# Two MLP layers on one Trainium2 core: seven block products for eight over batch pairs, with a fixed order of engines

## The chip, the cores and the metric

The kernel runs on one core of a Trainium2 chip. The time is the device time of one execution in microseconds. A core has a matrix engine (TensorE, PE in the rows; its weight loads are PEld), VectorE (DVE), ScalarE (ACT), GpSimd (POOL), and a sync engine (SP) that here only issues transfers.

## What is computed

Attention over 4 batches and 12 heads feeds two layers of the same width; all arithmetic is judged at float32.

```python
# q, k, v: (4, 12, 448, 64)
q_n, k_n = rmsnorm(q, g_q), rmsnorm(k, g_k)
attn = softmax(q_n @ k_n.T / 8) ; x = attn @ v          # -> (4, 448, 768)
xn = (x - mean) / sqrt(var + 1e-6) * g_ln               # layer 0
x  = x + relu(xn @ w_ch1) @ w_ch2                       # 768 -> 3072 -> 768
u  = x + (x.T @ U @ V).T                                # layer 1: mixing over tokens, rank 32
out = u + relu(u @ w_ch1') @ w_ch2'
```

The weights arrive as 64-bit floats and are narrowed on the core by integer operations on their two halves.

## The kernel before

Attention goes head by head with a software pipeline (`attention`, lines 229 to 499); beside it run, as generators that are advanced one step per stage, the scaling of finished batches (`scale`), the layer norm (`ln_stats`, `ln_apply`) and the first weights (`early`). The result of batch b lies transposed in `x[b]`, six blocks of 128 features by 448 tokens.

Each operand of the layers' matmuls is kept as a high and a low part, and every product is three matmuls: high by high, low by high, high by low. A layer is 12 steps of two hidden blocks (`G = 2`). In each step all four batches go by in turn. For a batch, `h_unit` makes one hidden block of 128 by 448 (6 blocks of inputs x 3 = 18 matmuls, L591), ACT writes its high part (L595) and VectorE its low part (L596). `o_unit` makes one of the six output blocks from the two hidden blocks of the batch before (2 x 3 = 6 matmuls, L605), and VectorE adds it to `x` (L607). That is 36 + 36 matmuls for a batch in a step, each 128x128 weights by 448 columns.

The weights of a step are used by all four batches: `w_load` fetches a tile of 128x768 in two halves from SP's queue (L517), `w_narrow` makes float32 of it (`narrow`, L80 to L87: one ACT operation for each half, two VectorE operations on the whole, two for each half), and `w_split` makes high and low parts on ACT (L531) and POOL (L532).

All tiles in PSUM come from one pool of eight banks. The scheduler of the framework orders each engine's instructions, within what the program pins (`keep_in_program_order`). In `mlps` each unit is followed by one to four steps of a side generator: the rest of batch 3's scaling and layer norm during the first step, and `mix` (the token mixing of layer 1) as soon as a batch has left layer 0. `mix` transposes `x` in groups of three blocks (L557), multiplies by U and by V (L566, L575), adds into `x` (L576) and splits the sum for layer 1 (L577, L578).

Of the kernel before, what the change touches and what calls it, by code (L numbers as in the profile page):

```python
# [11 lines left out]
U32 = mybir.dt.uint32  # L12
AF = mybir.ActivationFunctionType
# [13 lines left out]
NCH = NF // G  # L27
EPS = 1e-6
NX = 4
SN = 2  # L30
OS = "smpabn"
NB = 2
DL = 3
# [6 lines left out]

CLAMP = struct.unpack("<f", struct.pack("<I", 0x30100000))[0]

# [5 lines left out]
def build(tc, qkv, gg, g_ln, w1a, w2a, w1b, w2b, u_in, v_in, out):  # L48
    nc = tc.nc
    V, A, PL, PE = nc.vector, nc.scalar, nc.gpsimd, nc.tensor  # L50
    with ExitStack() as es:
        cpool = es.enter_context(tc.tile_pool(name="const", bufs=1))
        xpool = es.enter_context(tc.tile_pool(name="x", bufs=1))
        psum = es.enter_context(tc.tile_pool(name="ps", bufs=5, space=bass.MemoryType.PSUM))
        lpool = es.enter_context(tc.tile_pool(name="lt", bufs=4))
        rpool = es.enter_context(tc.tile_pool(name="raw", bufs=4))
        fpool = es.enter_context(tc.tile_pool(name="wf", bufs=2))
# [3 lines left out]
        cnt = [0]  # L61

        def bank(name, tag="ps"):
            cnt[0] += 1
            return psum.tile([P, 512], F32, tag=tag, name=f"{name}{cnt[0]}", bufs=8)
# [5 lines left out]
        def narrow(raws, f, hold=False):  # L71

            fu = f.bitcast(U32)
            parts, at = [], 0
            for r in raws:
                n = r.shape[1]
                parts.append((r[:, :, 1], r[:, :, 0], slice(at, at + n)))
                at += n
            for hi, lo, n in parts:
                A.activation(f[:, n], hi.bitcast(F32), AF.Abs, scale=2.0 ** -16)  # L80
            ins = V.tensor_scalar(f, f, CLAMP, None, ALU.max)  # L81
            if hold:
                tc.keep_in_program_order(ins)
            V.tensor_scalar(fu, fu, 4, 1, ALU.logical_shift_left, ALU.logical_shift_right)
            for hi, lo, n in parts:
                V.scalar_tensor_tensor(fu[:, n], lo, 29, fu[:, n], ALU.logical_shift_right, ALU.bitwise_or)  # L86
                V.scalar_tensor_tensor(fu[:, n], hi, 0x80000000, fu[:, n], ALU.bitwise_and, ALU.bitwise_or)  # L87
# [46 lines left out]
        xh, xl = {}, {}  # L134

        def norm_tiles(b, pool, again=True):
            if b in xh and not again:
                return xh[b], xl[b]
            xh[b] = pool.tile([P, KD, S], F32R, tag=f"xh{b}", name=f"xh{b}_{cnt[0]}")
            xl[b] = pool.tile([P, KD, S], F32R, tag=f"xl{b}", name=f"xl{b}_{cnt[0]}")  # L140
            return xh[b], xl[b]

        pin = tc.keep_in_program_order
# [9 lines left out]
        def ln_stats(b, pool=None):  # L153
# [6 lines left out]
            if b < B - 1:  # L160
                xs = lt("xs")
                for c in range(NC):
                    cs = slice(c * CP, (c + 1) * CP)
                    V.tensor_reduce(xs[:, cs], x[b][:, :, cs].rearrange("p k n -> p n k"), AX.X, ALU.add)
                    yield
                yield
                parts = [xs]
            else:
                for _ in range(3):
                    yield  # L170
                parts = [x[b][:, k, :] for k in range(KD)]
# [9 lines left out]
            for n in range(KD + 1 + lag):  # L181
# [3 lines left out]
                if n < KD:  # L185
                    odd = b == B - 1 and n % 2
                    sqs[n] = acc if n == 0 else bank("sq")[:, :S] if odd else lt(f"sq{n}", pool)
                    (V if b == B - 1 and n % 2 else PL).tensor_tensor(sqs[n], x[b][:, n, :], mu, ALU.subtract)
# [346 lines left out]
        def early():  # L535
            for u in range(2):
                w_load(u)
# [186 lines left out]
```

## Time and profile before

| | |
|---|---|
| three runs | 1827.44, 1832.0, 1840.74 us (median 1832.0) |
| profiled execution, span of its instructions | 1826.3 us; the page gives no time of its own beside it |
| busy: PE, DVE, ACT, POOL | 97%, 61%, 31%, 24% |
| chain that ended last | 79% PE, of it the two layers' matmuls (L605 and L591) 38% each |
| DMA | 116.52 MB, mean 64 GB/s |

Busy is the share of the span in which an engine executed. A matmul's own duration overlaps the next one's, so what a matmul costs in a row of them is read from the chain of waits, where each step is followed back to what released it. The granted clock is given as a share of full speed.

### The profile page before, as it was taken

What the parts mean: (1) busy time and instruction counts of PE and PEld (TensorE: products, weight loads), DVE (VectorE), ACT (ScalarE), POOL (GpSimd) and SP (SyncE); (2) the same over time, 40 slices, a digit from 0 to 9 for tenths busy, and PEclk for the clock granted to TensorE, in tenths of its full rate; (3) what the DMA queues carried; (4) which work ended last, traced back from release to release, by engine and by line L of the source; (5) the groups of instructions that cost most, each with busy time, mean ns of one, the idle gap of its engine ahead of it and who ended that gap; (6) DMA issues with size and microseconds to landing.
All of it is one profiled execution on the core that took longest, in us unless ns stands there. A gap on an engine that the chain in (4) does not pass through costs nothing.

```text
span 1826.3 us, 22748 instructions
## 1 busy us (share of the span) xinstructions
PE 1776.4 (97%) x8690; PEld 1556.3 (85%) x8690; DVE 1108.7 (61%) x1942; ACT 565.8 (31%) x1147; POOL 430.1 (24%) x307
## 2 busy tenths in 40 slices
PE   5999998899999999999999999999999999999999
PEld 4666665588999999999999988999999999999998
DVE  6768787869655646465555676555555466454633
ACT  6786776633121221122121244121221112111210
POOL 5445667433110110111010133210110101110100
PEclk9999999999999999999999999999999999999999
DMA  4453433412212211121112201111212122111103
GB/s 107 107 121 72 107 84 96 126 37 90 84 36 70 70 35 54 50 70 51 54 37 68 69 27 44 35 47 58 70 35 70 36 69 70 35 52 52 35 1 121
DMA packets 72990, 116.52 MB, mean 64 GB/s; under 512 B 30065, under 2 KB 42929, under 8 KB 72881
## 3 DMA queue, kind: packets, MB, share of 16 engines
q1 hardware_dynamic: 45232, 99.92, 19.0%
q10 hardware_dynamic: 27648, 15.14, 3.3%
q8 instruction: 68, 1.11, 0.3%
q14 instruction: 42, 0.34, 0.1%
HBM read 98.35 MB, written 5.68 MB: 57 GB/s over the span
## 4 chain that ended last, share of the span: by engine, by line
PE 79%; POOL 2%; DVE 2%; issue 2%; DMA 0%; ACT 0%; SPq 0%; POOLq 0%; DVEq 0%; ACTq 0%
PE o L605 38%; PE h L591 38%; PE po L399 1%; PE t L566 1%; PE xt L557 0%; POOL w L532 0%; DVE m L349 0%; POOL ln_d L222 0%; POOL xl L217 0%; DVE ln_acc L184 0%; POOL raw L287 0%; SPq L456 0%; DVE wf L86 0%; POOL xl L578 0%; PE mu L174 0%
## 5 line engine op out<-in xcount | busy, mean ns | idle before, releaser
L591 PE MATMUL h<-xh,w 128*128 128x448 f32 x2304 | 656.7, 366 | 2.6 <-ACT xh L216 2.6
L605 PE MATMUL o<-hh,w 128*128 128x448 f32 x2304 | 657.0, 366 | 0.0
L591 PEld LDWEIGHTS h<-xh,w 128*128 128x128 f32 x2304 | 433.7, 188 | 37.5 <-ACT xh L216 3.0
L605 PEld LDWEIGHTS o<-hh,w 128*128 128x128 f32 x2304 | 432.8, 188 | 35.0 <-issue 1.1
L607 DVE TENSOR_TENSOR x<-x,o 128x448 f32<-128x448 f32 x576 | 349.9, 617 | 158.8 <-PE o L605 155.6
L532 POOL TENSOR_TENSOR w<-wf,w 128x768 fp32r<-128x768 f32 x96 | 183.1, 1917 | 1056.8 <-ACT w L531 1056.8
L591 PE MATMUL h<-xl,w 128*128 128x448 f32 x1152 | 422.0, 366 | 0.6 <-POOL xl L217 0.5
L605 PE MATMUL o<-hl,w 128*128 128x448 f32 x1152 | 421.1, 366 | 0.0
L595 ACT ACTIVATE hh<-h 128x448 fp32r<-128x448 f32 x192 | 103.7, 540 | 794.3 <-PE h L591 794.3
L596 DVE SCALAR_TENSOR_TENSOR hl<-h,hh 128x448 fp32r<-128x448 f32 x192 | 119.3, 622 | 322.6 <-ACT hh L595 322.5
L591 PEld LDWEIGHTS h<-xl,w 128*128 128x128 f32 x1152 | 216.9, 188 | 19.3 <-POOL xl L217 2.2
L605 PEld LDWEIGHTS o<-hl,w 128*128 128x128 f32 x1152 | 216.7, 188 | 17.2
L399 PE MATMUL po<-p,vf 112*128 112x448 f32 x384 | 178.2, 547 | 2.1 <-DVE m L349 2.1
L349 DVE TENSOR_REDUCE m<-pm 112x1 f32<-112x448 f32 x192 | 118.0, 618 | 48.7 <-PE pm L348 48.0
L81 DVE TENSOR_SCALAR wf<-wf 128x768 f32<-128x768 f32 x96 | 67.9, 707 | 128.0 <-ACT wf L80 121.7
L80 ACT ACTIVATE wf<-wr 128x384 f32<-128x384 f32 x192 | 96.8, 549 | 148.0 <-POOL w L532 147.4
L86 DVE SCALAR_TENSOR_TENSOR wf<-wr,wf 128x384 uint32<-128x384 uint32 x192 | 122.9, 661 | 1.7
L531 ACT CAST w<-wf 128x768 fp32r<-128x768 f32 x96 | 77.8, 831 | 130.4 <-PE o L605 116.9
L87 DVE SCALAR_TENSOR_TENSOR wf<-wr,wf 128x384 uint32<-128x384 uint32 x192 | 112.1, 595 | 0.7
L378 ACT ACTIVATE p<-ps 112x448 f32<-112x448 f32 x192 | 104.2, 543 | 11.6 <-PE ps L375 11.1
L374 PE MATMUL ps<-bq,a 128*112 128x448 f32 x192 | 99.8, 520 | 2.9 <-DVE m L349 2.2
L399 PEld LDWEIGHTS po<-p,vf 112*128 112x128 f32 x384 | 74.3, 194 | 12.4 <-DVE m L349 2.5
(111 smaller groups left out, 1306.1 us busy)
## 6 DMA issues: line engine op xcount, KB each, us to landing
wr<-in_w1a SPq DMA_DIRECT2D x48, 384.0 KB
wr<-in_w2a SPq DMA_DIRECT2D x48, 384.0 KB
wr<-in_w1b SPq DMA_DIRECT2D x48, 384.0 KB
wr<-in_w2b SPq DMA_DIRECT2D x48, 384.0 KB
raw<-in_qkv ACTq DMA_DIRECT2D x42, 224.0 KB
vf<-in_qkv ACTq DMA_DIRECT2D x48, 112.0 KB
a<-a SPq DMA_DIRECT2D x48, 112.0 KB
x<-u SPq DMA_DIRECT2D x48, 112.0 KB
```

The source lines that it names most:

```text
L86: V.scalar_tensor_tensor(fu[:, n], lo, 29, fu[:, n], ALU.logical_shift_right, ALU.bitwise_or)
L87: V.scalar_tensor_tensor(fu[:, n], hi, 0x80000000, fu[:, n], ALU.bitwise_and, ALU.bitwise_or)
L349: V.tensor_reduce(m[:, c:c + 1], pm[:CP, :S], AX.X, ALU.max)
L374: PE.matmul(pb[:CP, :S], a1[:, cs], bq, start=True, stop=False)
L378: A.activation(p, pb[:CP, :S], AF.Exp)
L399: PE.matmul(po[:, :S], vf[:, j, c, :], ps[c], start=(c == 0), stop=(c == NC - 1))
L532: PL.tensor_tensor(lo, f, f32(hi), ALU.subtract)
L591: PE.matmul(ph[:, :S], wt[:, k, :], xt[:, k, :], start=(n == 0), stop=(n == 3 * KD - 1))
L595: A.activation(hh, ph[:, :S], AF.Relu)
L596: V.scalar_tensor_tensor(hl, ph[:, :S], 0.0, f32(hh), ALU.max, ALU.subtract)
L605: PE.matmul(po[:, :S], wt[:, e, :], ht, start=(n == 0), stop=(n == 3 * G - 1))
L607: V.tensor_tensor(x[b][:, e, :], x[b][:, e, :], po[:, :S], ALU.add)
```

## The change

One layer is now two passes of 12 steps, first over batches 0 and 1, then over 2 and 3. A step has the same two hidden blocks, for a pair of batches. In the first step of a pass, and in the whole first pass of layer 0, the hidden blocks are made as before (`h_unit`, 18 matmuls, four units). In every other step they come from seven products of 9 matmuls: the two hidden blocks by the two batches are a 2x2 block matrix, the 768 inputs are cut in halves, and sums of weight blocks (made on POOL) and sums of input blocks T1 to T4 (made on VectorE at the start of a pass) are multiplied instead of the blocks. The seven results lie in three accumulations X, Y and Z; ACT copies three of them out and VectorE adds them before the hidden parts are made. The second product is as before, 12 units of 6 matmuls for a pair. Further:
- Each layer's weights are used in two passes. A narrowed tile is stored to DRAM and fetched for the second pass; splitting is done in each pass. Layer 1's first weights are narrowed during layer 0's second pass.
- The normalised inputs are stored to DRAM; those of batches 2 and 3 are normalised during the first pass and fetched, through the ring `raw`, when the second begins.
- In the layers the program holds a list scheduler (`Op`, `work`, `on_pe`): every operation has an engine, a cost, what it reads and the slots that it takes and gives back; the engines' instructions are issued in the order so planned, and the framework keeps it. Slots come from rings of fixed size: 6 PSUM banks (two more are for the side work), 6 halves of second-layer weights, 5 pairs of hidden parts, 5 sums.
- The narrowing has two ACT and two VectorE operations for each half of a tile.
- Batch 3's layer norm sums its blocks on VectorE first, like the others'.

The core of the diff (`A` is ACT, `V` VectorE, `PL` POOL):

```diff
-            for hi, lo, n in parts:
-                A.activation(f[:, n], hi.bitcast(F32), AF.Abs, scale=2.0 ** -16)
-            ins = V.tensor_scalar(f, f, CLAMP, None, ALU.max)
-            if hold:
-                tc.keep_in_program_order(ins)
-            V.tensor_scalar(fu, fu, 4, 1, ALU.logical_shift_left, ALU.logical_shift_right)
-            for hi, lo, n in parts:
-                V.scalar_tensor_tensor(fu[:, n], lo, 29, fu[:, n], ALU.logical_shift_right, ALU.bitwise_or)
...
+        def bits(r, f):
+            A.activation(r[:, :, 0], r.bitcast(U8).rearrange("p n (t q) -> p n t q", t=2)[:, :, 0, 3], AF.Copy,
+                         scale=1.0 / 32, bias=-31.0 / 64)
...
+        def scaled(r, f):
+            A.activation(f, r[:, :, 1].bitcast(F32), AF.Abs, scale=2.0 ** -112)
...
+        def join(r, f):
+            f = f.bitcast(U32)
+            V.scalar_tensor_tensor(f, f, 3, r[:, :, 0], ALU.logical_shift_left, ALU.bitwise_or)
...
+        def sign(r, f):
+            f = f.bitcast(U32)
+            V.scalar_tensor_tensor(f, r[:, :, 1], 0x80000000, f, ALU.bitwise_and, ALU.bitwise_or)
...
+            yield
             pm = bank("mu")
-            for k, t in enumerate(parts):
-                pin(PE.matmul(pm[:, :S], ones_m, t, start=(k == 0), stop=(k == len(parts) - 1)))
...
             lag = 1 if tmp else 0
             for n in range(KD + 1 + lag):
                 k = n - 1 - lag
                 if k >= 0:
-                    pin(A.copy(h[:, k, :], d[k]))
-                    (V if b > 1 and k % 2 else PL).tensor_tensor(l[:, k, :], d[k], f32(h[:, k, :]), ALU.subtract)
+                    nc.sync.dma_start(xn[b][k], d[k])
...
+                        names = {k[0] for k in op.acq}
+                        t = None if waiting & names else op.start()
+                        waiting |= names
+                        if t is None or t >= until or (best and t >= best[0]):
+                            continue
+                        if t + op.cost <= first.get(op.eng, t + op.cost) + TOL:
+                            best = (t, q, n)
...
+        def on_pe(count, fn, ins=(), out=None, acq=(), rel=()):
+            work(clock[0])
+            t = clock[0]
...
+            t = max([clock[0]] + [ready[k] + LAT for k in ins] + [min(rings[k[0]])[0] + LAT for k in acq])
+            for k in acq:
+                take(k)
+            fn()
+            clock[0] = t + count * 203
+            if out:
+                ready[out] = clock[0] + 100
+            for k in rel:
+                give(k, clock[0])
...
+        def fetch(t):
+            layer, i = steps[t[0]][0], t[1]
+            where = "raw" if i and steps[t[0]][1] else "wf"
+            job(SP, 60, lambda: SP.dma_start(weights(t), wd[layer, i, feature(t)]), [("wd", layer, i, feature(t))],
+                ("wf", t), [(where, t)], land=4500)
...
+        def w2_forms(s, e):
+            for g in range(2):
+                t = (s, 1, g)
+                split(("w2", s, g, e), lambda t=t: halves(t)[e], [("wf", t)],
+                      [("raw" if steps[s][1] else "wf", t)] if e else ())
...
+            def add(k, p, q, op, ins):
+                job(PL, 1150, lambda: PL.tensor_tensor(at("s", s, k), p(), q(), op), ins, ("sum", s, k), [("s", s, k)])
...
+            split(("w", s, 0), h(0, 0), both)
+            yield
+            add(S1, h(1, 0), h(1, 1), ALU.add, both)
+            add(S2, get(S1), h(0, 0), ALU.subtract, done(S1))
+            split(("w", s, S1), get(S1), done(S1, S2), [("s", s, S1)])
+            add(S4, h(0, 1), get(S2), ALU.subtract, done(S2))
...
+        def prepare(s, i):
+            stored = steps[s][1] == 1 or (steps[s][0] == 1 and i == 0) or (s, i) == (0, 1)
+            for g in range(2):
+                (fetch if stored else narrow_jobs)((s, i, g))
...
+        def plain(s):
+            layer, pair, c = steps[s]
+            return c == 0 or layer == pair == 0
...
+            def source(layer, b, k, who):
+                if layer:
+                    return (lambda: x[b][:, k, :]), [("mixed", b)], []
...
+
+                job(SP, 60, lambda: SP.dma_start(tile_(), xn[b][k]), [("xn", b)], ("st",) + key, [key], land=3000)
+                return tile_, [("st",) + key], [key]
...
+                def split_t(to, n, name, ins=()):
+                    parts_of(to, k, t(n), [("t", n, p, k), *ins], name, p, [("tm", n, p, k)])
+
+                make(1, s12, s11, i12 + i11, r11)
+                make(3, s22, s12, i22 + [("t", 1, p, k)], r12)
+                make(2, s22, t(1), [("t", 3, p, k)], r22)
+                split_t(one[0, 1], 1, "T1", [("unit", s, 1, 1), ("t", 2, p, k)])
+                split_t(more[1], 3, "T3")
+                make(4, s21, t(2), i21 + [("t", 2, p, k)], r21)
+                split_t(more[0], 2, "T2", [("t", 4, p, k)])
+                split_t(more[2], 4, "T4")
...
+            def product(s, n):
+                new = n in (0, 1, 5)
+                to = ("bank", s, "XYXYXZX"[n])
+
+                def go():
+                    terms(at(*to), form(("w", s, n)), moving[n](), new, True)
+
+                before = {2: "c", 3: "s", 4: "r", 6: "s2"}.get(n)
+                on_pe(9, go, [("w", s, n)] + moved(names[n], steps[s][:2]) + ([(before, s)] if before else []),
+                      ("P", s, n), [to] if new else (), [("w", s, n)])
+                done = [("P", s, n)]
...
+
+                def plus(name, g, j, rel=()):
+                    def t():
+                        return at("tm", name, s)
+
+                    soon(V, 640, lambda: V.tensor_tensor(t(), t(), src, ALU.add),
+                         done + [(name, s)], (name + "2", s), rel=rel)
+                    hidden(s, g, j, t, [(name + "2", s)], [("tm", name, s)])
+
+                if n < 3:
+                    copy("csr"[n])
+                elif n == 3:
+                    plus("r", 0, 1, [to])
+                elif n == 4:
+                    plus("s", 1, 1)
+                elif n == 5:
+                    plus("c", 0, 0, [to])
+                else:
+                    hidden(s, 1, 0, lambda: src, done, [to])
+
...
+                done = [("w2", s, g, e // 3) for g in range(G)] if j == 0 and e % 3 == 2 else []
+                if e == KD - 1:
+                    done += [("h", s, g, j) for g in range(G)]
...
+                def add():
+                    V.tensor_tensor(x[b][:, e, :], x[b][:, e, :], at(*key)[:, :S], ALU.add)
+
+                soon(V, 640, add, [("o", s, e, j)], ("x", s, b, e), rel=[key])
...
+                std, last, nxt = plain(s), c == NCH - 1, s + 1 < NS
...
+                if c == 2 and layer != pair:
+                    side += [(heavy, 4, ("mixed", 2 * layer + j), mix(2 * layer + j)) for j in range(2)]
...
+                    move("wf", NWF - 1, "wx")
+                    move("raw", 2, "rx")
...
+                if c == 0 and s:
+                    for k in range(3):
+                        combos(s, (layer, pair), k)
...
+                if std:
+                    units = [lambda g=g, j=j: h_unit(s, g, j) for j in (1, 0) for g in range(2)]
+                    plan = [3, 3, 3, 3]
+                else:
+                    units = [lambda n=n: product(s, n) for n in range(7)]
+                    plan = [2, 2, 2, 2, 2, 1, 1]
...
+        ring("bank", tiles("bank", psum2, 6, [P, 512], F32))
```

## Rows read from the trace of the kernel before

**Rows 1.** Busy share of each engine, and busy tenths in 40 equal slices (the page).
```profile
PE 1776.4 (97%) x8690; PEld 1556.3 (85%) x8690; DVE 1108.7 (61%) x1942; ACT 565.8 (31%) x1147; POOL 430.1 (24%) x307
...
PE   5999998899999999999999999999999999999999
```

**Rows 2.** Chain of waits, layer 1: start us, us, engine, tile, line, instructions.
```profile
1144.02 7.30 PE h L591 x36
1151.31 7.29 PE o L605 x36
```

**Rows 3.** Table of stages: stretch, length, busy of PE, PEld, DVE, ACT, POOL; clock, DMA.
```profile
325.00:369.57 44.57, 39.51 (x160) 24.60 (x158) 37.32 (x61) 26.59 (x58) 16.30 (x11) 0.96 0.41 104
...
411.78:422.55 10.77, 7.55 (x21) 5.36 (x21) 10.73 (x16) 3.19 (x6) 6.98 (x5) 0.68 0.00 1
422.55:1046.12 623.57, 623.57 (x3078) 577.83 (x3077) 365.35 (x629) 125.54 (x224) 87.58 (x46) 1.00 0.20 61
...
1109.41:1144.02 34.61, 31.55 (x156) 28.36 (x156) 26.01 (x46) 14.85 (x30) 13.34 (x11) 0.90 0.15 46
1144.02:1822.56 678.54, 678.52 (x3348) 628.57 (x3347) 355.01 (x615) 120.08 (x216) 83.89 (x46) 1.00 0.17 52
```

**Rows 4.** Chain of waits, token mixing in the layer change.
```profile
1049.77 0.66 PE xt L557 x6
...
1054.73 2.11 PE t L566 x12
...
1063.90 0.41 PE u L575 x2
```

**Rows 5.** Chain of waits, batch 3's layer norm statistics.
```profile
389.53 3.01 PE mu L174 x8
...
393.75 1.66 PE mu L174 x4
...
406.35 0.75 PE var L196 x2
```

**Rows 6.** PE timeline at the first stumble (brackets: idle before), then the chain behind it.
```profile
414.58 1.12 PE L591 MATMUL h<-xh,w 128*128 128x448 f32 x2 [2.63 <-ACT xh L216]
...
418.89 7.07 PE h L591 x28
```

**Rows 7.** Waits of PE in the layers: us in total, times, longest.
```profile
PE t L566 <- DVE xl L560: 3.6, 4, 2.9
```

**Rows 8.** Groups by line: count, busy us, mean ns, idle before.
```profile
L607 DVE TENSOR_TENSOR x<-x,o 128x448 f32<-128x448 f32 x576 | 349.9, 617 | 158.8 <-PE o L605 155.6
L532 POOL TENSOR_TENSOR w<-wf,w 128x768 fp32r<-128x768 f32 x96 | 183.1, 1917 | 1056.8 <-ACT w L531 1056.8
L86 DVE SCALAR_TENSOR_TENSOR wf<-wr,wf 128x384 uint32<-128x384 uint32 x192 | 122.9, 661 | 1.7
...
L80 ACT ACTIVATE wf<-wr 128x384 f32<-128x384 f32 x192 | 96.8, 549 | 148.0 <-POOL w L532 147.4 <-DMA wr<-in_w1a 0.4 <-DMA wr<-in_w2a 0.2
L87 DVE SCALAR_TENSOR_TENSOR wf<-wr,wf 128x384 uint32<-128x384 uint32 x192 | 112.1, 595 | 0.7
...
L225 DVE SCALAR_TENSOR_TENSOR ln_d<-ln_d,gln,ln_acc 128x448 f32<-128x448 f32 x18 | 20.0, 1111 | 10.4 <-POOL ln_d L222 10.4
```

**Rows 9.** Chain of waits, small transfers in attention (SPq issues, DMA lands).
```profile
305.51 1.62 DMA rs<-sy
...
309.57 0.59 SPq L456
...
312.46 3.14 DMA r<-rs
```

**Rows 10.** DVE and POOL timelines near 456 us; L607 shortest, median, longest ns.
```profile
456.60 2.55 DVE L86 SCALAR_TENSOR_TENSOR wf<-wr,wf 128x384 uint32<-128x384 uint32 x2
...
456.04 2.23 POOL L532 TENSOR_TENSOR w<-wf,w 128x768 fp32r<-128x768 f32 x1 [2.77 <-ACT w L531]
...
L607 DVE TENSOR_TENSOR x<-x,o x576: 603/620/623, 387.4 to 1822.6; 128x448 f32<-128x448 f32 x192
```

More of the change, by code (lines that the diff above doesn't have):

```diff
@@ new lines, in build, with ring, tiles @@
+        FR = "p (k m) -> p k m"
+        SP = nc.sync
+        bufs, held, rings, ready = {}, {}, {}, {}
+        free = {A: 0, V: 0, PL: 0, SP: 0}
+        queues = ([], [], [])
+        clock = [0]
+        moves = {}
+        def ring(name, tiles):
+            bufs[name] = tiles
+            rings[name] = [(0, i) for i in range(len(tiles))]
+        def tiles(name, pool, n, shape, dt):
+            return [pool.tile(shape, dt, tag=f"{name}{i}", name=f"{name}{i}", bufs=1) for i in range(n)]
@@ new lines, in mix @@
+                    tl = lpool.tile([CP, HD], F32R, tag="lt", name=f"tl{b}_{hf}{c}")
+                    A.copy(th, px[:CP, :HD])
+                    yield
+                    V.tensor_tensor(tl, px[:CP, :HD], f32(th), ALU.subtract)
+                    yield
+                    for n, (w, t) in enumerate(((uh, th), (ul, th), (uh, tl))):
+                        PE.matmul(pt[:3 * R, :HD], w[:, c, :], t,
+                                  start=(c + n == 0), stop=(c == NC - 1 and n == 2))
+                    yield
@@ L588, in h_unit @@
                 n = 0
-                for k in range(KD):
-                    for wt, xt in ((hi, xh[b]), (lo, xh[b]), (hi, xl[b])):
-                        PE.matmul(ph[:, :S], wt[:, k, :], xt[:, k, :], start=(n == 0), stop=(n == 3 * KD - 1))
+                for k in range(3):
+                    for wt, xt in ((w[0], t[0]), (w[1], t[0]), (w[0], t[1])):
+                        PE.matmul(out[:, :S], wt[:, k, :], xt[:, k, :], start=(first and n == 0),
+                                  stop=(last and n == 8), skip_group_check=True)
@@ L665, in build, with moved, h_unit @@
-        pool = es.enter_context(tc.tile_pool(name="mlp", bufs=1, reuse_waits="tile"))
-        xpools.append(pool)
-        for n, _ in enumerate(ln_apply(2, xpools[2])):
-            next(last if n else most)
-        mlps(pool, [chain(most, last, ln_stats(B - 1), ln_apply(B - 1, pool))])
+            def moved(name, p):
+                return [(name, p, k) for k in range(3)]
+            def h_unit(s, g, j):
+                p = steps[s][:2]
+                key = ("bank", s, g, j)
+                def go():
+                    for r in range(2):
+                        terms(at(*key), form(("w", s, 2 * g + r)), one[r, j], r == 0, r == 1)
+                ws = [("w", s, 2 * g + r) for r in range(2)]
+                on_pe(18, go, ws + moved(f"0{j}", p) + moved(f"1{j}", p), ("unit", s, g, j), [key], [] if j else ws)
+                hidden(s, g, j, lambda: at(*key)[:, :S], [("unit", s, g, j)], [key])
@@ new lines, in mlps @@
+            for h in range(2):
+                for j in (1, 0):
+                    for e in range(3):
+                        o_unit(NS - 1, 3 * h + e, j)
+            work(clock[0] + 10 ** 6)
+            assert not queues[0] and not queues[1] and not side
+        wpool = es.enter_context(tc.tile_pool(name="ring", bufs=1))
+        ring("w", tiles("w", wpool, 6, [P, 2, 3, P], F32R))
+        with tc.tile_pool(name="raw", bufs=4) as rpool, tc.tile_pool(name="wf", bufs=3) as fpool:
+            with tc.tile_pool(name="ps", bufs=8, space=bass.MemoryType.PSUM) as psum:
+                banks.update(pool=psum, tag="ps", ps=8)
+                with tc.tile_pool(name="att", bufs=1, side="right") as ap:
+                    with tc.tile_pool(name="tok", bufs=1) as ep, tc.tile_pool(name="feat", bufs=1) as ep2:
+                        most, last = attention(ap, ep, ep2, early())
@@ L672 @@
+        raws, fs = tiles("raw", mpool, 4, [P, 3 * P, 2], U32), tiles("wf", mpool, NWF, [P, DM], F32)
+        first = ExitStack()
+        xpool = first.enter_context(tc.tile_pool(name="first", bufs=1, reuse_waits="tile"))
+        ring("raw", raws + tiles("raw_", xpool, 4, [P, 3 * P, 2], U32))
+        ring("wf", fs + tiles("wf_", xpool, 3, [P, DM], F32))
+        with tc.manual_schedule():
+            pins[0] = False
+            mlps(chain(most, last))
 _INS = ["qkv", "gg", "g_ln", "w1a", "w2a", "w1b", "w2b", "u", "v"]
```

522 lines of the change are left out of this document (346 added, 176 removed).

## The prediction

> **What bounds the kernel now.** I read the busy shares first, then the slices, then the chain of waits. TensorE is busy for 97% of the span and, after the first slice, in nearly every slice; the next engine, VectorE, stands at 61% [rows 1]. In the chain of waits almost the whole second half is one engine: blocks of 36 matmuls follow each other every 7.296 us (1151.31 less 1144.02 is 7.29, and 7.30 comes as often), so one 128x448 matmul takes 0.2027 us of the chain [rows 2]. From there on time is matmuls counted.
>
> The stage table cuts the span at 369.57 us, where the last attention matmuls give way to the first unit of the layers [rows 3]. From there to 1822.56 us are 1453.0 us. The two layers hold 6912 such matmuls (two layers, 12 steps, 4 batches, 36 + 36): 1400.9 us. The rest:
> - the token mixing between the layers. One batch costs TensorE 8 x 0.33 for transposes (0.66 is two groups), 2 x 2.11 for the low-rank product and 3 x 0.41 for the way back, 8.1 us, four times 32.4 [rows 4];
> - the layer norm statistics of batch 3, which sum six blocks with six matmuls: 3.01 + 1.66, and 0.75 for the variance, 5.4 us [rows 5];
> - two stumbles. At 411.78 us the next unit waits 2.63 us for batch 3's normalised input, and then runs partly at the lower of the two clock levels, 1.2 instead of 2.4 GHz (the stage's mean granted clock is 0.68) [rows 3, 6]. Its 36 matmuls end at 425.96 instead of 419.08: 6.9 us lost. In the layer change TensorE waits 3.6 us for VectorE's low parts [rows 7], and the stage after it has a mean clock of 0.90 over 34.6 us, another 3.5 us [rows 3]: 7.1 us.
> 1400.9 + 32.4 + 5.4 + 14.0 = 1452.7, against 1453.0 in the table. Nothing large is left unexplained, so what the change does to this phase can be summed.
>
> **What the change removes.** A plain step of a batch pair takes 4 first-product units of 18 matmuls and 12 second-product units of 6, 144. A seven-product step takes 7 x 9 + 72 = 135. The function that decides which steps are plain names the whole first pass and the first step of every other pass, so 3 x 11 = 33 steps save 9 matmuls: 297 x 0.2027 = 60.2 us. Batch 3's sum is folded on VectorE first, so one matmul is left for six; with the variance that is some 1.5 us instead of 5.4: 3.9 us. The stumble at 411.78 goes: the first pass works on batches 0 and 1 alone, and batch 3 has a pass of 350 us (12 x 29.2) to be normalised in. The one in the layer change goes too if the mixing, now spread over steps 2 and on of the next pass, waits for nothing: 14.0 us. Together 78.1 us, if nothing new waits.
>
> **What it adds.** Loads of the other engines per seven-product step (135 x 0.2027 = 27.4 us):
> - POOL: the weights are now split once per pair, in halves of 128x384, 11 of them, and 4 sums of blocks. A whole 128x768 split took 1917 ns [rows 8], a half some 0.96: 15 x 0.96 = 14.4 us, 53%, against 87.6 of 623.6 us (14%) before [rows 3].
> - VectorE: 12 + 3 additions at 617, 4 hidden parts at about the same, and in the two passes that still narrow two tiles, 8 narrowing operations at 0.60 to 0.66 [rows 8]: 16.8 us, 61%. In the first pass the narrowing is 16 operations, some 20 of 29.2 us.
> - ACT: narrowing needs two instructions for each half where it needed one (549 ns) [rows 8]; with copies and splits some 13.5 us, half the step.
> - SP and the queues: four weight tiles fetched (1.57 MB), two raw tiles (1.57 MB) and two stores (0.79 MB) is 143 GB/s; the stage before moved 61 GB/s at a DMA share of 0.20 [rows 3], so 0.47 by proportion. About ten issues of 0.59 us at most [rows 9] are 6 us of SP's step.
> None of these reaches TensorE's 27.4 us, so as means they are hidden. What isn't is order: every engine now runs its list as planned, and whoever waits holds what is behind it. Behind a waiting VectorE are the additions that free PSUM banks, of which there are six where there were eight; behind those, TensorE. I price the places where that can happen:
> - *Entry.* The first steps' weights are loaded, narrowed and split while the first 72 matmuls (14.6 us) run. From 0 to the 6.9 us of a stumble; I take 2.
> - *Layer 0, first to second pass.* This is the largest one. The sums T1 to T4 need, for each of three k, four tiles of batches 2 and 3 from DRAM, through a ring that was cut to two slots. Two loads go together, the third needs the slot of the second, the fourth that of the first. A load is between 0.59 + 1.62 and 0.59 + 3.14 us (the small transfer and the broadcast) [rows 9]; at 2.9 us, with some 3 us of subtracting and splitting, a round is 11 to 12 us and three are 35. TensorE asks for T1 in the second product of the next step, 29.2 + 4.2 = 33.4 us after the pass begins. So with free slots the wait is some 2 to 5 us. But the second-layer weights of that same step lie in that ring too and leave only when their second half is split, which needs a weight slot that the ninth second-product unit frees, 21.9 us into the step. If they hold these two slots, T1 comes at about 57 and TensorE waits 21 to 26 us, and then up to 3.5 more at the half clock. Which slots they hold depends on times in the plan that I can't see; I take 15, ends 2 and 30.
> - *The two pass changes of layer 1* read x in SBUF, with no loads. VectorE has 18 operations more in that step, 11 us on top of some 15, of 29.2: 0 to 5 each, 4 together.
> - *Mixing.* The same matmuls, each group emitted one or two units after its input; 32 groups with waits of 0 to at most the 2.9 us seen before [rows 7]. 0 to 12; I take 2.
> - *VectorE held by POOL.* See the third rival: 0 to 52; I take 2.
> - *Attention.* Narrowing there loses two VectorE passes per tile, and batch 2's normalisation moves out of its end, where VectorE is busy for 37.3 of 44.6 us and TensorE idles 5 [rows 3]; twelve stores of normalised tiles come onto SP, each waiting for VectorE with attention's copies behind it. -5 to +8; 0.
> Added: 25 us. Net 78 - 25 = 53.
>
> **The sum.** Span 1826.3 - 53 = 1773 us. The page gives no time of that execution beside its span; the three runs shown lie 1 to 14 us above it and their median 5.7. The same step on the median gives 1832 - 53 = 1779 us.
>
> **Rivals.**
> 1. *Everything new is covered*: 1832 - 78 = 1754 us. For it: busy means below 70% on every other engine, and 623 us before without one wait [rows 3]. Against it: the two-slot ring.
> 2. *The count isn't lower*, because more steps are plain than I read. Then only waits change, about 1832 - 18 + 25 = 1839, within 1%. Against it: the condition is two comparisons.
> 3. *VectorE's narrowing is held by POOL in every step.* At 456.04 a POOL split runs 2.23 us, and the two narrowing operations issued beside it take 2.55 us, where the mean of one is 0.66 [rows 8, 10]; the additions that read PSUM never take over 0.623 [rows 10]. In attention, with POOL over half busy, the normalising operation on SBUF alone averages 1111 ns [rows 8]. With POOL at 53% about one hold of 1.1 us a step that the six banks don't cover, 47 times, is 52 us: 1754 + 52 = 1806. Against it: 27.4 - 16.8 leaves VectorE 10 us of slack a step.
> The Trainium skill, SBUF — State Buffer, section "Who interferes with whom", says that a VectorE instruction with two SBUF inputs and a GpSimd instruction that reads SBUF exclude each other for a whole instruction. The trace agrees (2.55 us beside 2.23); by that rule the third rival's 1806 is the figure, while the mean of 661 ns that the row shows at POOL's old share would give the forecast.
> 4. *Slower: the shorter ring starves TensorE in short stops, each followed by a stretch at the half clock.* A stop of 2.63 us cost 6.9 us in all [rows 6]. With product banks held over several units three or four banks are left for second products; a late VectorE then stops TensorE in the same place of every step. One such stop in each of 33 steps is 228 us: 1754 + 228 = 1982. It decides from 12 such stops (78 / 6.9). For it: three additions per step are now links between products. Against it: between a product and the one that needs its copied sum lie 5 us of other matmuls, and one addition takes 0.62.
> The Trainium skill, TensorE: Matmul & The Clock Gate, section "A second HAM failure mode: psum-queue depth-cycling", describes this for a kernel that cycled through PSUM banks: the time lost in returning to full clock, not in the matmuls. No row before shows it with eight banks (clock 1.00 over 623 us); by it the sum would be rival 4.
>
> **How the numbers follow.** Forecast 0.57, rival 1 0.18, rival 3 0.14, rival 4 0.08, rival 2 0.03. The forecast is the likeliest case's 1779. From 1748 (rival 1 with attention's gain) to 1818 (rival 3 with the long pass change) the range leaves out rivals 2 and 4 and thin ends. A change under 1% (18 us) can't be told from none here: the runs shown spread 0.7%. Faster by more: 0.57 + 0.18 + half of rival 3, 0.82; within: the other half and rival 2, 0.10; slower: 0.08.
>
> **What would show it.** Right: 36 matmuls still in 7.30 us in most blocks, 6615 of them, clock 1.00 there; no wait at batch 3's input; one gap of 5 to 25 us some 370 us after the layers begin, waiting for a sum's low part; POOL near half busy. Wrong: gaps that repeat every 27 us (rivals 3 and 4, told apart by the clock), or an attention phase that ends over 10 us later or earlier than 369.6.

## The result, and the profile after

The changed kernel takes 1785.3 us (median of four runs, 1782.2 to 1786.7) against 1830.4 for the kernel before in the same runs: a ratio of 0.975, 95% interval 0.972 to 0.978. The forecast was 1779, in a range from 1748 to 1818. The profiled execution's span is 1784.8 us, 41.5 less than before. Its page first, the lines that answer to [rows 1]:

```profile
PE 1719.9 (96%) x8383; PEld 1499.0 (84%) x8383; DVE 1164.6 (65%) x1906; ACT 873.3 (49%) x1865; POOL 938.2 (53%) x841
...
PE   5999999989999999769999999999999999999999
...
DMA  3443444567644343444343443333323331122101
```

TensorE has 57 us less to do and still fills the span to 96%; POOL has gone from 24% to 53%. In the slices there is one dip that wasn't there before, in the seventeenth and eighteenth. The transfers have grown from 116.52 to 213.35 MB (third line, tenths of the DMA engines' time).

The chain of waits in the last pass, and at its end (start, us, tile, line, instructions):

```profile
1494.92 2.43 PE bank L938 x12
1497.35 1.82 PE bank L873 x9
...
1765.48 15.82 PE bank L938 x78
```

Nine matmuls in 1.82 us and twelve in 2.43: the price of a matmul is that of [rows 2]. The groups by line give their number:

```profile
L938 PE MATMUL bank<-h,w 128*128 128x448 f32 x3456 | 757.1, 367 | 0.0
...
L873 PE MATMUL bank<-xh,w 128*128 128x448 f32 x1512 | 435.0, 369 | 26.0 <-ACT xh L813 21.0 <-ACT w L657 3.2 <-POOL w L658 1.8
...
L873 PE MATMUL bank<-xl,w 128*128 128x448 f32 x756 | 278.3, 368 | 2.5 <-DVE xl L815 2.3
...
L873 PE MATMUL bank<-T,w 128*128 128x448 f32 x891 | 197.6, 366 | 0.0
```

1512 + 756 + 891 = 3159 of the first product and 3456 of the second: 6615, as counted. The layers begin where attention's last matmuls end, at 365.8 us (369.6 before), and end at 1765.48 + 15.82 = 1781.3: 1415.5 us against 1453.0.

The stages, to be read beside [rows 3] (stretch, length, busy of PE, PEld, DVE, ACT, POOL, clock, DMA share, GB/s):

```profile
365.82:386.11 20.29, 15.33 (x74) 13.46 (x73) 7.46 (x16) 9.52 (x22) 4.65 (x5) 0.94 0.84 296
...
531.10:732.77 201.67, 201.67 (x976) 182.88 (x975) 125.45 (x205) 82.76 (x175) 80.71 (x74) 1.00 0.43 145
732.77:780.40 47.63, 24.14 (x97) 19.62 (x97) 27.42 (x42) 17.48 (x36) 19.28 (x17) 0.71 0.54 171
780.40:1082.00 301.60, 301.60 (x1515) 278.09 (x1514) 200.38 (x315) 142.80 (x297) 169.71 (x158) 1.00 0.42 134
...
1466.00:1781.00 315.00, 315.00 (x1556) 291.82 (x1554) 133.92 (x222) 96.72 (x193) 168.32 (x155) 1.00 0.18 57
```

Two stretches aren't full: the entry (clock 0.94 over it, and the matmuls behind it at half clock) and the 47.6 us about the change from layer 0's first to its second pass, with TensorE busy for 24 us and a mean clock of 0.71. From 780 us on there is not one wait of TensorE. POOL is busy for 170 of 301.6 us there, 56%, and VectorE for 66%.

The gap in TensorE's timeline (brackets: idle before, released by):

```profile
749.45 0.67 PE L873 MATMUL bank<-xh,w 128*128 128x448 f32 x2 [1.19 <-ACT xh L813]
...
751.66 0.47 PE L873 MATMUL bank<-xl,w 128*128 128x448 f32 x1 [1.54 <-DVE xl L815]
...
764.28 1.11 PE L873 MATMUL bank<-xh,w 128*128 128x448 f32 x2 [12.15 <-ACT xh L813]
...
766.20 0.74 PE L873 MATMUL bank<-xl,w 128*128 128x448 f32 x1 [0.80 <-DVE xl L815]
...
774.63 1.11 PE L873 MATMUL bank<-xh,w 128*128 128x448 f32 x2 [7.69 <-ACT xh L813]
```

That is 23.4 us of waits, all for the high and low parts of T1, one k after the other; 21.0 us of them are for the high parts that ACT makes. What stands behind them, first SP's own list and then the chain:

```profile
731.13 0.32 SPq L826 DMA_DIRECT2D raw<-xn  x1
```

```profile
738.48 1.89 POOL w L658 x2
740.36 3.36 DMA raw<-xn
...
744.47 2.51 DMA raw<-xn
...
748.36 4.86 DMA raw<-xn
...
776.60 3.80 PE bank L938 x12
```

The load at 731.13 is the thirteenth of 24 of its kind, and the first for the sums: the twelve before it bring the inputs of the pass's first step, and it goes into the slot that the last of them left. T1 is the difference of two tiles, and the second tile has no slot yet. The two POOL operations at 738.48 are the splits of the second halves of the second-layer weights; the second load for the sums leaves SP at 740.36, on the heels of the first of them. The pass began at 714.2 us, so this is 26 us into it. Followed through `take` and `give` of the program's rings, one of the two weight tiles lies in one of the sums' two slots until that split; the other lies in a slot that goes to the narrowing ahead. Then loads of 2.4 to 4.9 us follow one another. The stretch from 732.77 to the end of the fourth second-product unit of the pass's second step, at 780.40, holds 96 matmuls, 19.5 us of work: 28.2 us lost, of it 23.4 in waits and most of the rest at half clock.

The entry (chain, then TensorE's timeline):

```profile
368.46 5.70 DMA raw<-in_w1a
...
374.17 6.78 DMA wf<-wd
...
381.46 0.84 POOL w L658
```

```profile
383.57 0.74 PE L873 MATMUL bank<-xh,w 128*128 128x448 f32 x1 [3.17 <-ACT w L657]
...
386.11 0.74 PE L873 MATMUL bank<-xh,w 128*128 128x448 f32 x1 [1.79 <-POOL w L658]
```

By 391.76 us 90 matmuls are done, 18.2 us of work in 25.9: 7.7 us lost. One more loss shows no wait at all. It lies in the pitch, the time from one matmul's start to the next one's. Two pieces of the chain, each 18 matmuls, at a granted clock of 1.00:

```profile
526.73 3.65 PE bank L873 x18
531.13 3.72 PE bank L938 x18
```

From 531 to 733 us the pitch is 0.2067 us instead of 0.2027. Over all pieces of the chain at this pitch the difference adds up to 4.4 us.

The balance of the layers: 6615 x 0.20267 = 1340.7, mixing 32.4, statistics 1.5, together 1374.6; entry 7.7, pass change 28.2, slower pitch 4.4: 1414.9 of 1415.5. Against the kernel before, the span's 41.5 us come out as 60.2 (the 297 matmuls) + 17.9 (stumbles and statistics) + 3.8 (attention ends earlier) - 28.2 - 7.7 - 4.4 = 41.6.

Last the groups of the other engines that answer to [rows 8] (count, busy us, mean ns, idle before), and two lines' shortest, median and longest ns:

```profile
L658 POOL TENSOR_TENSOR w<-wf,w 128x384 fp32r<-128x384 f32 x251 | 272.5, 1096 | 357.0 <-ACT w L657 342.4 <-issue 9.8 <-PE u L788 3.9
...
L80 DVE SCALAR_TENSOR_TENSOR wf<-raw,wf 128x384 uint32<-128x384 uint32 x184 | 134.9, 742 | 1.5
...
L76 DVE SCALAR_TENSOR_TENSOR wf<-wf,raw 128x384 uint32<-128x384 uint32 x184 | 127.1, 707 | 33.7 <-ACT raw L68 23.8 <-issue 4.5 <-ACT wf L72 3.1
...
L76 DVE SCALAR_TENSOR_TENSOR wf<-wf,raw x184: 542/553/1508, 376.1 to 1419.3; 128x384 uint32<-128x384 uint32 x184
...
L865 DVE SCALAR_TENSOR_TENSOR h<-tm,h x99: 616/620/1570, 788.3 to 1764.2; 128x448 fp32r<-128x448 f32 x99
```

### The profile page after: what moved, and what is told of

The parts are those of the page before. It is cut to its first block, busy times and chain, and to the rows that moved or that the text cites. A ratio compares the mean times of both kernels' runs of the same rounds, so it can differ in the third digit from the quotient of the medians.

```text
span 1784.8 us, 24102 instructions
## 1 busy us (share of the span) xinstructions
PE 1719.9 (96%) x8383; PEld 1499.0 (84%) x8383; DVE 1164.6 (65%) x1906; ACT 873.3 (49%) x1865; POOL 938.2 (53%) x841
## 2 busy tenths in 40 slices
DMA packets 111433, 213.35 MB, mean 120 GB/s; under 512 B 34448, under 2 KB 53456, under 8 KB 111312
## 4 chain that ended last, share of the span: by engine, by line
PE 78%; DMA 2%; DVE 2%; POOL 1%; issue 1%; ACT 0%; SPq 0%; DVEq 0%; POOLq 0%; ACTq 0%
PE bank L938 39%; PE bank L873 35%; PE po L386 1%; DMA raw<-xn 1%; PE t L777 1%; PE xt L767 1%; DMA wf<-wd 0%; PE ps L361 0%; POOL ln_sq L177 0%; DMA raw<-in_w1a 0%; PE ps L362 0%; POOL w L658 0%; PE u L788 0%; PE pm L335 0%; DVE m L336 0%
## 5 line engine op out<-in xcount | busy, mean ns | idle before, releaser
L938 PE MATMUL bank<-h,w 128*128 128x448 f32 x3456 | 757.1, 367 | 0.0
L938 PEld LDWEIGHTS bank<-h,w 128*128 128x128 f32 x3456 | 648.9, 188 | 53.6 <-issue 0.4
L949 DVE TENSOR_TENSOR x<-x,bank 128x448 f32<-128x448 f32 x576 | 353.5, 618 | 342.2 <-PE bank L938 337.3
L658 POOL TENSOR_TENSOR w<-wf,w 128x384 fp32r<-128x384 f32 x251 | 272.5, 1096 | 357.0 <-ACT w L657 342.4
L873 PE MATMUL bank<-xh,w 128*128 128x448 f32 x1512 | 435.0, 369 | 26.0 <-ACT xh L813 21.0
L873 PEld LDWEIGHTS bank<-xh,w 128*128 128x128 f32 x1512 | 284.9, 189 | 52.5 <-ACT xh L813 22.2
L873 PE MATMUL bank<-xl,w 128*128 128x448 f32 x756 | 278.3, 368 | 2.5 <-DVE xl L815 2.3
L873 PE MATMUL bank<-T,w 128*128 128x448 f32 x891 | 197.6, 366 | 0.0
L873 PEld LDWEIGHTS bank<-T,w 128*128 128x128 f32 x891 | 166.7, 188 | 13.0
L873 PEld LDWEIGHTS bank<-xl,w 128*128 128x128 f32 x756 | 142.8, 189 | 16.0 <-DVE xl L815 4.1
```

What stands on the lines that cost most here:

```text
L658: job(PL, 1100, lambda: PL.tensor_tensor(form(key)[1], src(), f32(form(key)[0]), ALU.subtract), [("hi",) + key], key, rel=rel)
L873: PE.matmul(out[:, :S], wt[:, k, :], xt[:, k, :], start=(first and n == 0), stop=(last and n == 8), skip_group_check=True)
L938: PE.matmul(at(*key)[:, :S], wt[:, e % 3, :], t, start=(n == 0), stop=(n == 3 * G - 1))
L949: V.tensor_tensor(x[b][:, e, :], x[b][:, e, :], at(*key)[:, :S], ALU.add)
```

## The experiments

Theory S: the gap at the pass change is the staging ring `raw`, cut to two slots, where weights hold a slot until the ninth second-product unit. Rival Q: the loads are slow because the queues also carry the narrowing ahead. For the entry: the fetch of the first second-layer weights against SP's start and the narrowing chain. For the rest: whether counting matmuls is enough, or the links, the banks or the narrowing have a price or a share of their own.

**e1_four_slots**
```diff
                     move("wf", NWF - 1, "wx")
+                if (layer, pair, c) == (0, 1, 1):
                     move("raw", 2, "rx")
```


> The staging ring keeps its four slots through the first step of layer 0's second pass; only then are two given to the narrowing ahead. Theory S (slots): the gap of 28 us comes from the two slots being held by that step's second-layer weights until the ninth second-product unit. The first load for the sums then starts some 8 us into the pass instead of 34, the gap falls from 28 to between 3 and 10 us, the time to about 1765. Rival Q (queues): the loads are slow because the transfer engines carry the narrowing ahead as well (share 0.54 there); the narrowing is only moved by a step, so the gap stays above 18 us and the time above 1775.

Measured: 1767.9 us, ratio to the kernel before 0.9645 (0.960 to 0.969), span 1766.1. Both waits of over 7 us have become one of 6.6; with the small ones 8.0 us are left:

```profile
754.18 1.11 PE L873 MATMUL bank<-xh,w 128*128 128x448 f32 x2 [6.57 <-ACT xh L813]
```

S holds, as far as the ring goes: the first load for the sums leaves at 718.85 us, 7 us into the pass for 8 expected, though in the changed kernel the first two leave 17 and 26 us into the pass and not the 34 that the expectation names. The edit gives 18.7 us of span; some of that is pitch (the slower one costs 1.3 us here, for 4.4). It also moves the loads for the narrowing ahead by a step, because the ring that they use exists only then; e2 moves these loads alone. Four slots with those loads left in place were not tried.

**e2_no_ahead_loads**
```diff
-                if (layer, pair) == (0, 1):
-                    for g in range(2):
-                        narrow_jobs((s + NCH, 0, g), True)
+                if (layer, pair) == (0, 1) and c:
+                    for v in (s - 1, s) if c == 1 else (s,):
+                        for g in range(2):
+                            narrow_jobs((v + NCH, 0, g), True)
```


> Slots as in the changed kernel, but the raw tiles that are narrowed ahead in the first step of that pass are asked for a step later, so their loads no longer share the queues with the loads for the sums. S: the gap keeps its 28 us within 4. Q: it falls below 15 us.

Measured: 1790.4 us (one run), span 1788.5. The waits are 2.5, 9.2 and 11.4 us, 23.0 for 23.4:

```profile
764.54 1.12 PE L873 MATMUL bank<-xh,w 128*128 128x448 f32 x2 [9.18 <-ACT xh L813]
...
778.06 1.11 PE L873 MATMUL bank<-xh,w 128*128 128x448 f32 x2 [11.35 <-ACT xh L813]
```

Q falls: with those loads out of the way and the ring as it was, the gap stays.

**e3_entry_order**
```diff
-                weights_of(s + 2, s + 1)
+                if s:
+                    weights_of(s + 2, s + 1)
...
                     f()
+                    if s == 0 and i == 1:
+                        weights_of(2, 1)
```


> The weights of step 2 are asked for after two units of step 0 instead of before its first, so that the fetch of the first second-layer weights is no longer behind their loads. Theory: that fetch, landing at 381 us, is what the two waits of 3.2 and 1.8 us at the entry go back to; the entry's loss falls from 7.7 us to under 2 and the span by some 6. Rival: SP's late start (its first weight load goes out at 368 us, after attention's last transfers) and the chain of narrowing set it; the loss stays over 5 us.

Measured: 1783.2 us (one run), span 1781.3; the waits at the entry are 3.07 and 1.69 us, for 3.17 and 1.79. The 3.5 us less of span are about what the slower pitch takes less here (0.6 us, for 4.4). The edit tests nothing, since SP's list is the same: eight loads and then the fetch. In the plan the fetch waits for a slot of `wf` behind the narrowing that is queued ahead of it, and SP takes the later loads first.

```profile
367.51 5.51 SPq L638 DMA_DIRECT2D raw<-in_w1a  x8
373.12 0.90 SPq L615 DMA_DIRECT2D wf<-wd  x2
```

**e4_eight_products**
```diff
         def plain(s):
             layer, pair, c = steps[s]
-            return c == 0 or layer == pair == 0
+            return True
...
-                if c == 0 and s:
-                    for k in range(3):
-                        combos(s, (layer, pair), k)
```
(and `o_unit` no longer waits for the sums)

> All steps plain, nothing else undone: two passes, the planned order, the six banks, the new narrowing stay; no sums of inputs or weights are made. Count theory: 297 matmuls come back (+60 us), the gap of 28 us goes with the sums: about 1817 us. Rival: the links between the seven products cost TensorE time that the trace doesn't show as waits (a slower pitch, half clock), so that a plain step is dearer by less than 1.83 us: under 1805.

Measured: 1830.8 us, ratio to the kernel before 0.9995 (0.997 to 1.002), span 1827.5: 14 us above the expected 1817, and 10.7 above the 1816.8 that 1784.8 + 60.2 - 28.2 gives for the span. The pass change shows no wait. Its layers begin at 368.4 us, 2.6 later than the changed kernel's, and 2942 matmuls run at the slower pitch, which costs 12.0 us by the same sum as above, 7.6 more:

```profile
1022.97 3.72 PE bank L873 x18
1026.69 3.72 PE bank L938 x18
```

1784.8 + 60.2 - 28.2 + 2.6 + 7.6 = 1827.0. So the count holds, and the rival with a hidden price of the links falls: no piece of the product chain is dearer than its matmuls. It also says that everything else in the change together (two passes, the planned order, the narrowing, six banks) comes to nothing against the kernel before. That is a balance and not an absence: the stumbles and statistics that are gone (17.9 us) are used up by the entry, whose waits are 3.1 and 2.0 us here too, and by the 12.0 us of pitch. Of these parts only the narrowing (e7) was tried alone. Of the 42.7 us of span between this run and the changed kernel 32.0 are the matmuls less the gap; the other 10.2 are pitch and an earlier begin of the layers, which nothing here ties to the seven products.

**e5_fetch_first**
```diff
+            if s == 0:
+                prepare(s, 1)
             if u < NS:
                 prepare(u, 0)
-            if s < NS:
+            if 0 < s < NS:
                 prepare(s, 1)
```


> The edit of the entry before this one left the order on SP as it was: the fetch waited in the plan for a slot behind the first narrowing. Here the fetch of the first second-layer weights is asked for ahead of step 1's loads. In the changed kernel ACT stands idle until it lands at 381 us, with the splits that TensorE waits for behind it. Theory: it lands by 376 us, the two waits (3.2 and 1.8 us) and the half clock after them go, the span falls by 5 to 8 us. Rival: step 1's own raw loads and narrowing are as late; then the same waits stand at the entry, against another producer, and the span moves by less than 2 us.

Measured: 1784.7 us (one run), span 1782.8, 2.0 less. The fetch lands by 372.4 us, and the entry is no better: waits of 2.63 and 2.64 us. ACT now idles for step 1's raw halves instead (the split of the fetched tile, and behind it the first narrowing):

```profile
372.44 0.51 ACT L657 CAST w<-wf 128x384 fp32r<-128x384 f32 x1 [1.56 <-DMA wf<-wd]
376.27 0.54 ACT L72 ACTIVATE wf<-raw 128x384 f32<-128x384 f32 x1 [3.32 <-DMA raw<-in_w1a]
378.13 0.55 ACT L72 ACTIVATE wf<-raw 128x384 f32<-128x384 f32 x1 [1.31 <-DMA raw<-in_w1a]
```

The theory of the entry falls; the rival's prediction came out.

**e6_five_banks**
```diff
-        ring("bank", tiles("bank", psum2, 6, [P, 512], F32))
+        ring("bank", tiles("bank", psum2, 5, [P, 512], F32))
```


> One bank less in the layers' PSUM ring (five for six), all else as in the changed kernel. If the links between products and the additions have slack, as the missing waits say, the span grows by less than 12 us. If the ring of six is near its edge (the fourth rival), short stops appear in every step, each with a stretch at half clock, and the span grows by over 60 us.

Measured: 1788.4 us (one run), span 1786.3, 1.5 above the changed kernel, which is within what the pitch alone moves. There is one stop of 1.53 us for an addition early in the first pass, and no wait of TensorE after the pass change. The fourth rival isn't near.

```profile
423.07 3.88 PE L938 MATMUL bank<-h,w 128*128 128x448 f32 x18 [1.53 <-DVE x L949]
```

**e7_narrowing_alone**: the kernel before with the functions `bits`, `scaled`, `join`, `sign` and the new `narrow`.
```diff
-                narrow(raws.pop(u), fs[u], 2 * G <= u < 4 * G)
+                narrow(raws.pop(u), fs[u])
```


> The kernel before with the change's narrowing alone (two ACT and two VectorE operations for each half). TensorE is the bound and VectorE off its path except at the end of attention: the layers' phase stays at 1453 us within 3, the attention phase may end up to 4 us earlier; ratio between 0.995 and 1.002. Rival: the narrowing gives a good part of the gain; ratio under 0.99.

Measured: 1836.9 us, ratio 1.0045 (1.001 to 1.008): slightly slower, above the 0.995 to 1.002 that I expected, though the interval reaches into it. VectorE is busy for 113 us less (995.8 for 1108.7), and TensorE waits 4.8 us for one of the blocks of batch 3 ahead of its layer norm, where the kernel before has no such wait:

```profile
PE mu L178 <- DVE x L463: 4.8, 1, 4.8
...
PE h L595 <- ACT xh L220: 2.6, 1, 2.6
```

That the narrowing alone gives the kernel before no time is shown; why the scheduler then placed batch 3's scaling later wasn't followed.

**e8_slots_and_fetch**: the edits of e1 and e5 together.

> Four staging slots through the first step of the pass, and the fetch ahead. If the two are independent the gains add: 18.7 us from the slots and 5 to 8 from the entry, span 1758 to 1762 us, time about 1762, ratio to the kernel before about 0.962. If one gives the other back later, the time stays at 1768.

Measured: 1771.0 us, ratio 0.965 (0.962 to 0.968), span 1768.2, for 1758 to 1762 expected. The pass change is as in e1 (6.55 us the longest wait), the entry keeps 1.9 and 2.6 us, and the slower pitch takes 5.2 us, 3.9 more than in e1. The fetch adds nothing, as e5 said; against e1 no difference can be told.

**e9_four_raw_at_entry**: the edit of e5, and
```diff
+        rings["raw"] = rings["raw"][:4]
...
                 if s == 1:
+                    rings["raw"] += [(clock[0], i) for i in range(4, 8)]
```


> The fetch first, and the raw ring held at four slots during step 0, so that step 2's four loads wait for the narrowing of step 1's tiles and can't share the queues with them. If the entry is late because eight tiles land together (the first raw halves at 376 and 378 us, five to seven after their issue), step 1's halves land by 375 and the waits at the entry (2.6 and 2.6 us) fall to under 1 together, the span to about 1776. If it is SP's start after attention's last transfers and the length of the narrowing chain, they stay above 3.

Measured: 1790.6 us (one run), span 1788.6. Step 1's halves land 2 us earlier (ACT's first two narrowing operations below, at 376.27 and 378.13 in e5), and the waits are still 2.22 and 2.63 us; a stop of 1.5 us at 505, which the changed kernel doesn't have, was not followed to its cause. The slower pitch takes 6.4 us here.

```profile
373.63 0.55 ACT L72 ACTIVATE wf<-raw 128x384 f32<-128x384 f32 x1 [2.31 <-DMA raw<-in_w1a]
376.44 0.54 ACT L72 ACTIVATE wf<-raw 128x384 f32<-128x384 f32 x1 [2.26 <-DMA raw<-in_w1a]
```

```profile
382.19 0.47 PE L875 MATMUL bank<-xh,w 128*128 128x448 f32 x1 [2.22 <-ACT w L657]
...
385.29 0.74 PE L875 MATMUL bank<-xh,w 128*128 128x448 f32 x1 [2.63 <-POOL w L658]
```

So neither the fetch nor the crowd of loads sets the entry. What stands in all these runs (the changed kernel, e3, e5, e8, e9) is SP's first load for the layers at 367.5 to 368.9 us, right behind attention's last transfers, and the chain of narrowing and splits behind it on ACT and POOL; which of its links decides wasn't tried.

**e10_sums_before_weights**: the edit of e1, and
```diff
-                weights_of(s + 2, s + 1)
+                if (layer, pair, c) == (0, 1, 0):
+                    prepare(s, 1)
+                    w2_forms(s, 0)
+                    w2_forms(s, 1)
+                weights_of(s + 2, NS if (layer, pair, c) == (0, 0, NCH - 1) else s + 1)
```


> Four staging slots through the first step of the pass, and that step's second-layer weights asked for behind the sums instead of ahead, so that no weight tile holds a slot while the sums' sources are staged. Theory S: the rounds then run two at a time from the first microseconds of the step and the gap (8 us of waits, some 3 of half clock with four slots) falls below 4; in exchange the second-layer weights could be late at the next step's first second-product unit, a wait of 0 to 5. Span 1756 to 1764 against 1766.1. If the gap stays at 8, the sums' own chain on ACT, VectorE and POOL sets it.

Measured: 1761.1 us (one run), span 1759.3. No wait of TensorE over 0.3 us is left at the pass change; its stretch is full (columns as in the stages above). The layers begin at 370.3 us here, 4.5 later than in the changed kernel, with the same source for attention.

```profile
730.00:780.00 50.00, 50.00 (x250) 46.26 (x249) 34.54 (x53) 24.34 (x51) 34.98 (x33) 1.00 0.48 155
```

**e11_all_three**: the edits of e5, e9 and e10.

> All of it: four slots, weights behind the sums, fetch first with four raw slots in step 0. With the entry's loss of 7.7 us and the pass change's 28 gone the sum is 1784.8 less 30 to 35, a span of 1750 to 1755, time about 1755, ratio to the kernel before about 0.959; the slower of the two pitches seen at full clock can give back 1 to 5.

Measured: 1759.6 us (1759.2 to 1763.5, six runs), ratio 0.960 (0.957 to 0.963), span 1757.5. The stages of its entry, first pass, pass change and the pass after it:

```profile
366.31:391.00 24.69, 20.79 (x89) 18.34 (x88) 14.63 (x21) 11.86 (x26) 11.36 (x9) 0.87 0.70 222
391.00:730.00 339.00, 336.43 (x1652) 309.69 (x1651) 247.08 (x396) 152.63 (x326) 135.47 (x120) 1.00 0.50 173
730.00:780.00 50.00, 49.80 (x247) 45.72 (x246) 33.43 (x51) 25.23 (x55) 36.04 (x34) 1.00 0.49 156
780.00:1080.00 300.00, 300.00 (x1507) 276.98 (x1506) 216.67 (x340) 148.97 (x310) 173.99 (x155) 1.00 0.46 146
```

In the stretch of the pass change TensorE is busy for 49.8 of 50 us at full clock; the entry still loses at clock 0.87. The span is 2.5 us above the end of what I expected, which counted the entry's 7.7 us as gained against what e5 and e9 show. This is the fastest version, 26 us below the changed kernel; e10's one run can't be told from it.

## Why the prediction was right

The likeliest case came, and its parts in order:
- *What is removed* was right to the microsecond: 6615 matmuls at 0.2027 us, the statistics and both stumbles of [rows 3, 5 to 7] gone, 78 us. e4 is the test of the count: with the 297 matmuls back, and no sums, the span is within 0.5 us of what they add up to.
- *The pass change* is the step where the chain of reasons held and the middle value didn't. I saw that the second-layer weights lie in the sums' ring until the ninth unit, priced the gap then at 21 to 26 us and up to 3.5 of half clock, and took 15 because I couldn't tell which slots they hold. They hold one of the two, not both, and that is enough: the other slot first passes the last inputs of the first step and then keeps one source of T1, which is of no use without the second. From there the estimate held: three rounds took 34 us, for 35, and TensorE went on 60 us into the pass, for 57. The waits are 23.4 us, 28.2 in all, and mostly for high parts, where I named a low part as the sign. e1, e2 and e10 show the mechanism: it moves with the ring and with the order of the weights, and not with the narrowing's loads alone.
- *The entry* cost 7.7 us, above the end that I gave (6.9) and far from the 2 that I took. Its cause is only narrowed down (e5, e9).
- *The other added terms* were too dear: both pass changes of layer 1, the mixing and POOL's holds were 8 us in my sum, and no wait of TensorE shows them. A half of a weight split took 1.10 us and not the 0.96 that I worked out, so POOL stands at 56% for 53. The holds are there. Narrowing operations reach 1508 ns beside a median of 553, hidden parts made from SBUF 1570 beside 620, and the mean of the narrowing rose to 707 and 742 from 661 and 595 [rows 8]. The longest of each ran beside a POOL operation that had begun 0.4 us before it. No wait of TensorE follows from 780 us on, where VectorE is busy for 66%.
The Trainium skill, SBUF — State Buffer, section "Who interferes with whom", has a VectorE instruction with two SBUF inputs and a GpSimd instruction that reads SBUF shut each other out. The trace agrees with the holds (the longest 1508 and 1570 ns against medians of 553 and 620), but no wait of TensorE shows a price, against the 52 us of the third rival.
- *The fourth rival* is out with a margin: no wait from 780 us on, and a bank less shows 1.5 us of span in one run. The Trainium skill, TensorE: Matmul & The Clock Gate, section "A second HAM failure mode: psum-queue depth-cycling", describes a matrix engine that loses its clock between groups while it cycles through PSUM; nothing of it shows here with six banks or five (granted clock 1.00 in all stages from 780 us on).
- *Attention* ended 3.8 us earlier, for 0. I don't count it to the change: in the kernels with the same attention source the layers began anywhere between 365.3 and 370.3 us.
- *Not foreseen*: the slower pitch, 4.4 us.

The differences from the 53 us forecast: 28.2 - 15 and 7.7 - 2 and 4.4 lost, some 8 and 4 won: about 12 us less gain in span than forecast, 41.5. The mechanism came as told; that the time lies within 7 us of the forecast is in part luck, since 23 us of losses that were priced too low or not at all stand against 12 of costs that didn't come.

## What to carry to other kernels

When one engine is full and nothing waits, a change that saves work on it can be priced by counting its instructions at their pitch in the chain of waits; the error then lies only in the few places where the work changes over. Look there at each ring of buffers that two streams share: what holds a slot, what frees it, and whether that comes behind the work that needs it; here 28 of 78 us went into one slot that came free too late, four slots gave 18.7 us of span back and another order of the loads with them 25.5. A fixed order that keeps the bound engine fed shows that by waits of nought, and that is worth looking for before its steps are tuned.

## What the runs showed of the hardware

The same 128x448 matmuls with a weight load each run at one of two pitches, 0.2027 or 0.2067 us, at a granted clock of 1.00 in both. A stretch at the slower one lasts from a few microseconds to over 400 (e4, from 1391 us to the end), and those followed here began or ended behind the entry, at a short stop or at a matmul of another kind (530.2 us: the statistics). In two kernels with the old layer loop, before and e7, it doesn't occur at all; in those with the new one it takes between 0.6 and 12.0 us. It differs between versions whose code there is the same (0.6 us in e3, 4.4 in the changed kernel), so differences of up to some 10 us in span between versions of this kernel can come from it alone. There is one profile of each version, so whether it also differs between executions of one version isn't shown. What chooses the pitch stays open.

After stops of 2.6 us and more in the layers the matmuls ran at about half clock, 0.37 us each, at once as in [rows 6] or from the third matmul on (e7, 422 us). After the stops of 1.24 to 1.56 us early in the first pass (e6, e9, e11) the clock held.
